# Attention and a gated FFN in one kernel: scaled values made with the second score unit, evenly spaced attention bursts, and a start with the second batch's attention moved into the first FFN chunk

## The chip, the cores and the metric

The kernel runs on one core of a Trainium2 chip. The metric is the device time of one execution in microseconds (us). Several executions of each kernel are timed, and one execution of each is profiled. The span of a profile, from the first to the last instruction, is about 2 us shorter than the time of the same execution.

## The reference

```python
# attention, per batch b and head h: B = H = 8, S = 576, D = 64
scores = q @ k^T / sqrt(D) + cum[i] - cum[j]     # cum = cumsum(log(clip(f)))
attn   = softmax(scores, causal)
o      = attn @ v
# FFN on x = o with heads side by side: 4608 tokens x 512
out = (sigmoid(x @ w_gate) * (x @ w_val)) @ w_out     # 512 -> 1536 -> 512
```

The kernel writes exp(cum[i] - cum[j]) as a factor for i, which cancels in the softmax, and a factor g[j] = exp(-cum[j]), shifted by a constant. It multiplies v by g; the result, `vg`, is "the scaled values" of this text.

## The kernel before

Heads are worked on in pairs; there are 32 pairs, four to a batch. A pair's scores are computed transposed (keys on partitions) in four units A, B, C and D, because the causal triangle is cut into pieces that fit PSUM banks. Each unit goes through PE (scores), ACT (exp) and POOL (causal mask). Then the AV stage on PE multiplies by `vg` and, for the row sums, by `g`.

```python
def Q_exp(p, u, sc):                      # unit u of pair p, scores in banks sc, sc+1
    e = esb.tile(...)
    nc.scalar.activation(e, ps[:, sc:sc + 2, 0:w], Exp, scale=scale)
    nc.gpsimd.affine_select(out=m, in_=m, ...)            # mask, on POOL

def vg_step(p):
    nc.gpsimd.tensor_tensor(out=vg, in0=vb[...], in1=g_bf[...], op=mult)   # on POOL

def AV_mm(p, b0, b1, b2):                 # outputs in b0, b1; row sums in b0, b2
    av(p, CH0, b0, C0, False)             # needs vg, eA, eC
    av(p, CH0, b0, 0, True); av(p, CH1, b2, 0, True)
    av(p, CH1, b1, 0, False)              # needs eB, eD as well
def norm_r(...)   # DVE: transposes of the row sums, reciprocal, transpose back
def norm_m(...)   # DVE: xT = output (b0, b1) * R, the "output multiply"
```

PE does the FFN in chunks of 512 tokens, nine in all. A chunk is 36 groups of four matmuls: 24 groups for gate and value, then 12 for the output. Between groups PE takes up attention work of the next batch, in "bursts" (`later` is emptied after the next FFN group):

```python
def burst1(p):
    Q_mm(p, "C", 2); Q_mm(p, "A", 0); Q_exp(p, "C", 2)
    later.append(lambda: Q_exp(p, "A", 0))
def burst2(p):
    Q_mm(p, "B", 2); Q_mm(p, "D", 0); Q_exp(p, "B", 2)
    later.append(lambda: (Q_exp(p, "D", 0), vg_step(p)))      # vg last
def burst3(p):
    T_step(p + 1, "k", 3, nc.scalar.copy); T_step(p + 1, "q", 4, nc.scalar.copy)
    AV_mm(p, 0, 1, 2); norm_r(p, 0, 1, 2)
    later.append(lambda: norm_m(p, 0, 1, 2))

# start: pairs 0..3 (batch 0) without FFN; early_pair(p) also transposes pair p+1
early_pair(0); load_w1(1); early_pair(1)
load_qk(1, 0, 1); load_v(1, 0)
early_pair(2); load_w1(2); early_pair(3); early_av(3)
burst1(4); flush(); burst2(4); flush()
load_qk(1, 1, 1); load_v(1, 1)
bursts = {0: burst3, 4: burst1, 7: burst2}   # position within nine FFN groups
for c in range(NTC):
    for s, grp in enumerate(ffn_groups(c)):
        ...                                   # loads; burst if s % 9 is in bursts
        grp(); flush()
```

So the FFN groups between bursts number 4 (AV to burst 1), 3 (burst 1 to burst 2) and 2 (burst 2 to AV).

The softmax here doesn't subtract the row's maximum and nothing guards it: scores larger than these inputs give would overflow.

Of the kernel before, what the change touches and what calls it, by code (L numbers as in the profile page):

```python
# [15 lines left out]
def kernel(  # L16
# [11 lines left out]
    nc = tc.nc  # L28
    B, H, S, D = q.shape
# [6 lines left out]
    HPAIR = H // 2  # L36
# [47 lines left out]
    def load_qk(b, hf, npiece):  # L84
        key = (b, hf)
        qt = qk_pool.tile([QP, 4, TPP * D], BF16, tag="qt", name="qt")
        kt = qk_pool.tile([QP, 4, TPP * D], BF16, tag="kt_in", name="kt_in")
        w = 4 // npiece
        for s in range(npiece):
            for src, dst in ((q, qt), (k, kt)):  # L90
                hs = slice(4 * hf + w * s, 4 * hf + w * s + w)
                nc.gpsimd.dma_start(
                    dst[:, w * s:w * s + w, :],
                    src[b, hs].rearrange("h (p t) d -> p h (t d)", t=TPP))
        qtiles[key], ktiles[key] = qt, kt

    def load_v(b, hf):
        vb = vbs[(2 * b + hf) % NVB]
        for h in range(4):
            nc.sync.dma_start(  # L100
                vb[:, 0:NJT - 1, h, :],
                v[b, 4 * hf + h, 0:(NJT - 1) * NP, :].rearrange("(t p) d -> p t d", p=NP))
        nc.sync.dma_start(
            vb[0:TAIL, NJT - 1, :, :],
            v[b, 4 * hf:4 * hf + 4, (NJT - 1) * NP:S, :].rearrange("h p d -> p h d"))

    def load_w1(gi):
        cs = slice(gi * 512, gi * 512 + 512)
        for src, dst in ((moe_w_gate, wg_bf), (moe_w_val, wv_bf)):
            nc.gpsimd.dma_start(dst[:, :, cs],  # L110
                                src.rearrange("(m p) c -> p m c", p=NP)[:, :, cs])

    def load_w2(gi):
        nc.gpsimd.dma_start(
            wo_bf[:, 4 * gi:4 * gi + 4, :],
            moe_w_out.rearrange("(m p) c -> p m c", p=NP)[:, 4 * gi:4 * gi + 4, :])
# [3 lines left out]
    later = []  # L120

    def flush():
        while later:
            later.pop(0)()

    def half_of(p):
        b, a = divmod(p, HPAIR)
        return b, a // 2, 2 * (a % 2)

    def T_step(p, which, bk, copy):  # L130
        b, hf, ho = half_of(p)
        src = (qtiles if which == "q" else ktiles)[(b, hf)]
        bank = ps[:, bk, 0:S // 2].bitcast(BF16)
        for t in range(TPP):
            for h in range(2):
                nc.tensor.transpose(  # L136
                    bank[64 * h:64 * h + 64, t * QP:(t + 1) * QP],
                    src[:, ho + h, t * D:(t + 1) * D], ident_bf[0:QP, 0:QP])
        if which == "q":
            dst = asb.tile([128, S], BF16, tag="qT", name="qT")  # L140
        else:
            dst = kts[p % NKT]
        st[p, which] = dst
        copy(dst[:, 0:S].rearrange("p (n t) -> p n t", t=TPP),  # L144
             bank.rearrange("p (t n) -> p n t", t=TPP))
# [10 lines left out]
    def Q_mm(p, u, sc):  # L156
        qT, kT = st[p, "q"], st[p, "k"]
        for jt, i0, i1, c in UNITS[u]:
            for h in range(2):
                hp = slice(64 * h, 64 * h + 64)  # L160
                nc.tensor.matmul(ps[:, sc + h, c:c + i1 - i0],  # L161
                                 kT[hp, jt * NP:(jt + 1) * NP], qT[hp, i0:i1],
                                 start=True, stop=True)

    def Q_exp(p, u, sc):
        w = UW[u]
        e = esb.tile([128, 2, 512], BF16, tag="e" + u, name="e" + u)
        st[p, u] = e
        nc.scalar.activation(e[:, :, 0:w], ps[:, sc:sc + 2, 0:w], ACTF.Exp, scale=scale)  # L169
        if u == "A":  # L170
            m = e.rearrange("p h (x c) -> p h x c", x=2)[:, :, :, 0:NP]
            pat = [[0, 2], [0, 2], [1, NP]]
        elif u == "B":
            m = e[0:TAIL, :, 320:320 + TAIL]
            pat = [[0, 2], [1, TAIL]]
        else:
            m = e[:, :, 0:NP]
            pat = [[0, 2], [1, NP]]
        nc.gpsimd.affine_select(out=m, in_=m, compare_op=ALU.is_ge, fill=0.0,  # L179
                                base=0, pattern=pat, channel_multiplier=-1)  # L180

    def vg_step(p):
        b, hf, ho = half_of(p)
        vb = vbs[(2 * b + hf) % NVB]
        vg = asb.tile([128, NJT, 2, D], BF16, tag="vg", name="vg")
        st[p, "vg"] = vg
        nc.gpsimd.tensor_tensor(  # L187
            out=vg, in0=vb[:, :, ho:ho + 2, :],
            in1=g_bf[:, :, 2 * p:2 * p + 2].unsqueeze(3).to_broadcast([128, NJT, 2, D]),
            op=ALU.mult)  # L190
# [19 lines left out]
    def AV_mm(p, b0, b1, b2):  # L210
        av(p, CH0, b0, C0, False)
        av(p, CH0, b0, 0, True)
        av(p, CH1, b2, 0, True)
        av(p, CH1, b1, 0, False)

    def norm_r(p, b0, b1, b2):
        NB = S // 32
        Z = nsb.tile([128, S], FP32, tag="Z", name="Z")
        nc.vector.transpose(Z[:, 0:C0], ps[:, b0, 0:C0])  # L219
        nc.vector.transpose(Z[:, C0:S], ps[:, b2, 0:C1])  # L220
        r = nsb.tile([128, NB], FP32, tag="r", name="r")
        nc.vector.reciprocal(r, Z.rearrange("p (n c) -> p n c", c=32)[:, :, 0])
        R = nsb.tile([128, S], FP32, tag="R", name="R")
        nc.vector.transpose(R.rearrange("p (n c) -> p n c", c=32),  # L224
                            r.unsqueeze(2).to_broadcast([128, NB, 32]))
        st[p, "R"] = R

    def norm_m(p, b0, b1, b2):
        b, a = divmod(p, HPAIR)
        psf = ps.rearrange("p b c -> p (b c)")  # L230
        o = b0 * 512 + C0
        nc.vector.tensor_tensor(out=xT[:, a, b * S:(b + 1) * S], in0=psf[:, o:o + S],  # L232
                                in1=st[p, "R"], op=ALU.mult)


    def early_pair(p):
        Q_mm(p, "A", 0)
        Q_exp(p, "A", 0)
        Q_mm(p, "C", 2)
        Q_exp(p, "C", 2)  # L240
        T_step(p + 1, "q", 4, nc.scalar.copy)
        T_step(p + 1, "k", 7, nc.vector.tensor_copy)
        vg_step(p)
        if p:
            early_av(p - 1)
        Q_mm(p, "B", 0)
        Q_exp(p, "B", 0)
        Q_mm(p, "D", 2)
        Q_exp(p, "D", 2)

    def early_av(p):
        AV_mm(p, 5, 6, 7)
        norm_r(p, 5, 6, 7)
        norm_m(p, 5, 6, 7)


    def burst1(p):
        if p >= NPAIR:
            return
        Q_mm(p, "C", 2)  # L260
        Q_mm(p, "A", 0)
        Q_exp(p, "C", 2)
        later.append(lambda: Q_exp(p, "A", 0))

    def burst2(p):
        if p >= NPAIR:
            return
        Q_mm(p, "B", 2)
        Q_mm(p, "D", 0)
        Q_exp(p, "B", 2)  # L270
        later.append(lambda: (Q_exp(p, "D", 0), vg_step(p)))

    def burst3(p):
        if p >= NPAIR:
# [55 lines left out]
    nc.sync.dma_start(f_nat, f.rearrange("b h s -> (b h) s"))  # L330
    load_qk(0, 0, 2)
    make_identity(nc, ident_bf)
    make_identity(nc, ident_f)
    load_qk(0, 1, 2)
    for i in range(NVB):
        nc.vector.memset(vbs[i][TAIL:NP, NJT - 1, :, :], 0.0)
    for i in range(NKT):
        nc.vector.memset(kts[i][:, S:SPAD], 0.0)
    nc.vector.memset(g_bf[TAIL:NP, NJT - 1, :], 0.0)
    load_v(0, 0)  # L340
    load_v(0, 1)

    nc.vector.tensor_scalar(out=f_nat, in0=f_nat, scalar1=1e-4, scalar2=1.0,
                            op0=ALU.max, op1=ALU.min)
# [10 lines left out]
    nc.vector.tensor_copy(g_bf[:, 0:NJT - 1, :], gps[:, 0:NJT - 1, :])  # L355
    nc.vector.tensor_copy(g_bf[0:TAIL, NJT - 1, :], gps[0:TAIL, NJT - 1, :])

    load_w1(0)
    early_pair(0)
    load_w1(1)  # L360
    early_pair(1)
    load_qk(1, 0, 1)
    load_v(1, 0)
    early_pair(2)
    load_w1(2)
    early_pair(3)
    early_av(3)
    burst1(4)
    flush()
    burst2(4)  # L370
    flush()
    load_qk(1, 1, 1)
    load_v(1, 1)

    bursts = {0: burst3, 4: burst1, 7: burst2}
    for c in range(NTC):
        P = HPAIR * (c + 1)
        for s, grp in enumerate(ffn_groups(c)):
            if c == 0 and s in (2, 5, 8):
                load_w2(s // 3)  # L380
            if s in ((2, 20) if c else (12, 26)) and c + 2 < B:
                load_qk(c + 2, int(s >= 20), 1)
                load_v(c + 2, int(s >= 20))
            x, y = divmod(s, 9)
            if y in bursts:
                bursts[y](P + x + (y > 0))
            grp()
            flush()

# [29 lines left out]
```

## Time and profile before

| | before |
|---|---|
| median time, 4 runs | 451.72 us (449.46 to 453.02) |
| span of the profiled run | 447.9 us |
| first FFN matmul | 46.93 us |
| a chunk with four pairs of attention | 48.38 us |
| a chunk without attention | 31.08 us |

From the page of the kernel before: the first line is an engine's busy time, its share and its instructions; the others show the busy share in 40 equal slices of the span, in tenths, and the granted TensorE clock in tenths of full speed.

```profile
PE 396.7 (89%) x3349; PEld 197.7 (44%) x3349; DVE 167.9 (37%) x283; ACT 221.0 (49%) x335; POOL 126.9 (28%) x213
...
PE   4726998999899989999899989998999988999996
...
PEclk9968899999999999999999999999999999999999
```

PE is the engine that bounds the kernel from the fifth slice on, but it keeps dropping from 9 to 8. The four stretches below are the start, chunk 0, chunk 1 and a chunk without attention (after the times: busy us of PE, PEld, DVE, ACT and POOL with instruction counts, then granted clock, DMA share and GB/s).

```profile
0.00:46.93 46.93, 25.36 (x349) 18.12 (x350) 19.36 (x39) 23.19 (x31) 29.03 (x52) 0.86 1.06 178
46.93:95.38 48.45, 44.78 (x402) 21.98 (x400) 18.72 (x31) 26.26 (x40) 17.37 (x28) 1.00 0.59 100
95.38:143.76 48.38, 44.71 (x402) 22.00 (x400) 19.02 (x33) 26.26 (x40) 14.57 (x24) 1.00 0.36 70
381.75:412.83 31.08, 31.08 (x146) 14.07 (x145) 8.26 (x12) 9.55 (x16) 0.00 (x0) 1.00 0.09 34
```

In chunk 1 PE is idle for 48.38 - 44.71 = 3.67 us, and no other engine is over 55% busy. What PE waits for after 47 us is in the list of waits: `vg`, 25.8 us in 27 waits, the longest 1.5 us. What PE waits for after 47 us is in the list of waits (total us, number of waits, longest): first for the matmul row, then, from the same list for the weight-load row, the same wait.

```profile
PE ps L206 <- POOL vg L187: 25.8, 27, 1.5
...
PEld L206 <- POOL vg L187: 29.8, 27, 1.8
```

One pair in the timeline (start, duration, engine, line, operation; in brackets the idle time before it and what ended it) shows why `vg` is late.

```profile
150.36 0.64 POOL L179 TENSOR_SCALAR_AFFINE_SELECT eA<-eA 128x512 bf16<-128x512 bf16 x1 [1.18 <-ACT eA L169]
...
152.70 0.41 POOL L179 TENSOR_SCALAR_AFFINE_SELECT eD<-eD 128x256 bf16<-128x256 bf16 x1 [0.30 <-ACT eD L169]
...
153.03 0.42 PE L136 MATMUL ps<-ident_bf,qt 96*64 96x96 bf16 x12
153.08 1.27 POOL L187 TENSOR_TENSOR vg<-vb_89,g_bf 128x640 bf16<-128x640 f32 x1
...
154.40 0.30 PE L206 MATMUL ps<-eA,vg 128*64 128x256 bf16 x2 [0.95 <-POOL vg L187]
```

POOL had nothing to do between the mask of eA (done at 151.00) and the mask of eB (152.11), but `vg` stands in its queue behind the last mask. The Trainium skill's page "Perfetto Trace Analysis", section "Tensor Engine Instruction (MATMUL, LD_WEIGHTS)", calls the execution queues of ACT, DVE and GpSimd (POOL here) strictly first in, first out, and the trace agrees: the 1.11 us of idle time ahead of the mask of eB went unused, and `vg` ran last. PE is through with its transposes at 153.45 and waits for `vg` until 154.40. The chain of waits over another pair shows the same from the other side (start, us, what):

```profile
104.21 0.39 POOL eD L179
104.60 1.25 POOL vg L187
105.85 0.04 issue
105.89 1.56 PE ps L206 x28
```

The mask of eD and `vg` lie on the chain that ended last, and the AV stage that follows takes 1.56 us in it.

### The profile page before, as it was taken

Reading aid. Unit: us, or ns where it says so; the run is one execution under the profiler, and the core shown is the slowest. Engines: PE = TensorE matmul, PEld = TensorE weight load, DVE = VectorE, ACT = ScalarE, POOL = GpSimd, SP = SyncE. Lnnn points to the kernel's source line nnn. Section 1 sums busy time; section 2 is a strip of 40 time slices with the busy share of each in tenths; the row PEclk is TensorE's granted clock in tenths of the full one; section 3 lists DMA queues with packets and bytes.
Section 4 is the critical chain, followed back from the end, with each engine's and each line's share of the span. In section 5 each row is a group of like instructions: output and inputs, shape, how many; then the busy total and the mean of one; then the engine's idle time right before and its main releaser. Section 6 shows DMA issues by size and latency. Waiting matters only on the chain.

```text
span 447.9 us, 8234 instructions
## 1 busy us (share of the span) xinstructions
PE 396.7 (89%) x3349; PEld 197.7 (44%) x3349; DVE 167.9 (37%) x283; ACT 221.0 (49%) x335; POOL 126.9 (28%) x213
## 2 busy tenths in 40 slices
PE   4726998999899989999899989998999988999996
PEld 2514444444444444444444444444444444444442
DVE  4524444234432444244423443244324442340330
ACT  5634455455555555455555554555545542332321
POOL 7753342432323233232323232323221121000000
PEclk9968899999999999999999999999999999999999
DMA  9998890573313703181317230370410001101002
GB/s 167 196 194 163 127 174 1 101 138 70 44 34 91 133 8 55 72 152 31 55 48 144 63 51 28 93 134 5 67 58 25 0 1 48 47 1 70 23 2 94
DMA packets 61061, 33.70 MB, mean 75 GB/s; under 512 B 39456, under 2 KB 56352, under 8 KB 61024
## 3 DMA queue, kind: packets, MB, share of 16 engines
q0 software_dynamic: 17616, 14.16, 21.7%
q1 hardware_dynamic: 43408, 19.03, 16.6%
q8 instruction: 26, 0.43, 0.4%
q14 instruction: 11, 0.09, 0.1%
HBM read 37.90 MB, written 9.44 MB: 106 GB/s over the span
## 4 chain that ended last, share of the span: by engine, by line
PE 66%; POOL 12%; ACT 8%; issue 8%; DMA 4%; DVE 1%; POOLq 0%; ACTq 0%
PE ps L300 33%; PE ps L315 16%; PE ps L206 11%; POOL vg L187 8%; PE ps L161 5%; ACT eB L169 4%; DMA kt_in<-in_k_dram 4%; ACT eC L169 2%; POOL eB L179 2%; POOL eD L179 2%; ACT eA L169 2%; POOL eA L179 1%; PE ps L136 1%; DVE kt_87 L144 1%; DMA out_dram<-ob 0%
## 5 line engine op out<-in xcount | busy, mean ns | idle before, releaser
L305 ACT ACTIVATE sg<-ps 128x512 bf16<-128x512 f32 x108 | 64.5, 597 | 120.8 <-PE ps L300 120.8
L307 DVE SCALAR_TENSOR_TENSOR gv<-sg,ps 128x512 bf16<-128x512 bf16 x108 | 74.3, 688 | 122.8 <-PE ps L300 120.9
L300 PE MATMUL ps<-xT,wg_bf 128*128 128x512 bf16 x432 | 111.3, 380 | 0.0
L300 PE MATMUL ps<-xT,wv_bf 128*128 128x512 bf16 x432 | 111.1, 380 | 0.0
L315 PE MATMUL ps<-wo_bf,gv 128*128 128x512 bf16 x432 | 99.2, 380 | 0.0
L300 PEld LDWEIGHTS <-wv_bf 128*128 128x128 bf16 x432 | 40.6, 98 | 49.4 <-issue 2.4
L315 PEld LDWEIGHTS <-gv 128*128 128x128 bf16 x432 | 40.1, 98 | 49.0 <-issue 3.2
L300 PEld LDWEIGHTS <-wg_bf 128*128 128x128 bf16 x432 | 39.4, 98 | 48.7 <-issue 4.1
L179 POOL TENSOR_SCALAR_AFFINE_SELECT eC<-eC 128x256 bf16<-128x256 bf16 x32 | 13.1, 409 | 163.1 <-ACT eC L169 163.1
L219 DVE STREAM_TRANSPOSE Z<-ps 128x256 f32<-128x256 f32 x32 | 14.4, 449 | 117.0 <-PE ps L206 117.0
L319 ACT ACTIVATE ob<-ps 128x512 f32<-128x512 f32 x36 | 21.5, 597 | 58.4 <-PE ps L315 55.1
L206 PE MATMUL ps<-eA,vg 128*64 128x192 bf16 (+1 forms) x128 | 18.3, 280 | 28.3 <-POOL vg L187 27.4
L206 PEld LDWEIGHTS <-vg 128*64 128x64 bf16 x448 | 23.4, 114 | 34.9 <-POOL vg L187 31.5
L169 ACT ACTIVATE eC<-ps 128x896 bf16<-128x896 f32 x32 | 29.3, 915 | 14.1 <-PE ps L161 14.1
L169 ACT ACTIVATE eB<-ps 128x768 bf16<-128x768 f32 x32 | 25.9, 811 | 20.1 <-PE ps L161 20.1
L169 ACT ACTIVATE eA<-ps 128x896 bf16<-128x896 f32 x32 | 29.3, 914 | 1.4 <-PE ps L161 1.4
L179 POOL TENSOR_SCALAR_AFFINE_SELECT eA<-eA 128x512 bf16<-128x512 bf16 x32 | 20.5, 641 | 23.4 <-ACT eA L169 23.4
L224 DVE STREAM_TRANSPOSE R<-r 128x576 f32<-128x576 f32 x32 | 24.9, 778 | 1.1
L232 DVE TENSOR_TENSOR xT<-ps,R 128x576 bf16<-128x576 f32 x32 | 24.2, 756 | 2.6
L136 PE MATMUL ps<-ident_bf,qt 96*64 96x96 bf16 x384 | 14.6, 216 | 11.0 <-DMA qt<-in_q_dram 5.7
L206 PEld LDWEIGHTS <-g_bf 128*64 128x64 bf16 x448 | 22.5, 116 | 3.2 <-issue 1.3
L144 ACT COPY qT<-ps 128x576 bf16<-128x576 bf16 x32 | 20.8, 651 | 5.3 <-PE ps L136 5.3
(55 smaller groups left out, 352.1 us busy)
## 6 DMA issues: line engine op xcount, KB each, us to landing
out_dram<-ob SPq DMA_DIRECT2D x36, 256.0 KB, 2.0
qt<-in_q_dram POOLq DMA_DIRECT2D x14, 288.0 KB, 5.5
kt_in<-in_k_dram POOLq DMA_DIRECT2D x14, 288.0 KB, 6.9
vb_89<-in_v_dram SPq DMA_DIRECT2D x24, 128.0 KB, 5.6
vb_90<-in_v_dram SPq DMA_DIRECT2D x20, 128.0 KB, 5.6
vb_91<-in_v_dram SPq DMA_DIRECT2D x20, 128.0 KB, 5.8
wg_bf<-in_moe_w_gate_dram POOLq DMA_DIRECT2D x3, 512.0 KB, 10.2
wv_bf<-in_moe_w_val_dram POOLq DMA_DIRECT2D x3, 512.0 KB, 12.7
```

The source lines that it names most:

```text
L144: copy(dst[:, 0:S].rearrange("p (n t) -> p n t", t=TPP), bank.rearrange("p (t n) -> p n t", t=TPP))
L161: nc.tensor.matmul(ps[:, sc + h, c:c + i1 - i0], kT[hp, jt * NP:(jt + 1) * NP], qT[hp, i0:i1], start=True, stop=True)
L169: nc.scalar.activation(e[:, :, 0:w], ps[:, sc:sc + 2, 0:w], ACTF.Exp, scale=scale)
L179: nc.gpsimd.affine_select(out=m, in_=m, compare_op=ALU.is_ge, fill=0.0, base=0, pattern=pat, channel_multiplier=-1)
L187: nc.gpsimd.tensor_tensor(out=vg, in0=vb[:, :, ho:ho + 2, :], in1=g_bf[:, :, 2 * p:2 * p + 2].unsqueeze(3).to_broadcast([128, NJT, 2, D]), ...
L206: nc.tensor.matmul(ps[64 * h:64 * h + 64, bank, off + oc:off + oc + w], lhsT, st[p, u][:, h, c:c + w], start=(x == 0), stop=(x == n - 1), ...
L224: nc.vector.transpose(R.rearrange("p (n c) -> p n c", c=32), r.unsqueeze(2).to_broadcast([128, NB, 32]))
L232: nc.vector.tensor_tensor(out=xT[:, a, b * S:(b + 1) * S], in0=psf[:, o:o + S], in1=st[p, "R"], op=ALU.mult)
L300: nc.tensor.matmul(ps[:, bk, :], w[:, mt, ft * NP:(ft + 1) * NP], xT[:, mt, t0:t0 + TCH], start=(mt == 0), stop=(mt == NMT - 1))
L305: nc.scalar.activation(sg, ps[:, bk, :], ACTF.Tanh, scale=0.5)
L307: nc.vector.scalar_tensor_tensor(out=gv[:, ft, :], in0=hold["sg"], scalar=1.0, in1=ps[:, bk, :], op0=ALU.add, op1=ALU.mult)
L315: nc.tensor.matmul(ps[:, bk, :], gv[:, ft, tt * NP:(tt + 1) * NP], wo_bf[:, ft, :], start=(ft == 0), stop=(ft == NFT - 1))
```

## The change

The change is meant to take `vg` off the critical path by queueing it on POOL right behind the mask of eA (the second score unit that a pair puts on PE), to space the bursts of chunks 1 and later evenly (three FFN groups between two bursts, but for one gap of two and one of four), and to start the FFN sooner: the second batch's attention is no longer begun ahead of the FFN but in the later part of chunk 0, one burst every two groups. Loads are reordered to suit (the first weights sooner, the loads of later batches at later groups of a chunk), and those of v for batch 1 are held back by tiny memsets on POOL ("gates").

```diff
+    def load_v(b, hf, gate=None):
+        if gate is not None:
+            for h in range(4):
+                gate.memset(vb[0:1, 0, h, 0:1], 0.0)
 ...
 def early_pair(p):
-        T_step(p + 1, "q", 4, nc.scalar.copy)
-        T_step(p + 1, "k", 7, nc.vector.tensor_copy)
+        if p + 1 < HPAIR:
+            T_step(p + 1, "q", 4, nc.scalar.copy if p % 2 else nc.vector.tensor_copy)
+            T_step(p + 1, "k", 7, nc.vector.tensor_copy)
 ...
+    def burst0(p):
+        T_step(p, "k", 3, nc.scalar.copy)
+        T_step(p, "q", 4, nc.scalar.copy)
 def burst1(p):
-        later.append(lambda: Q_exp(p, "A", 0))
+        later.append(lambda: (Q_exp(p, "A", 0), vg_step(p)))
 def burst2(p):
-        later.append(lambda: (Q_exp(p, "D", 0), vg_step(p)))
+        later.append(lambda: Q_exp(p, "D", 0))
 ...  (the identities, the first loads and the loads of later batches are moved)
     load_qk(1, 0, 1)
-    load_v(1, 0)
+    load_v(1, 0, nc.gpsimd)
 ...
+    load_qk(1, 1, 1)
+    load_v(1, 1, nc.gpsimd)
     early_av(3)
-    burst1(4)
-    flush()
-    burst2(4)
-    flush()
-    load_qk(1, 1, 1)
-    load_v(1, 1)
-    bursts = {0: burst3, 4: burst1, 7: burst2}
+    # chunk 0:  burst0 at group 9, then bursts 1, 2, 3, 1, ... at
+    pos = [10, 12, 14, 16, 18, 20, 22, 24, 26, 28, 30, 32]
+    # chunks 1 and later:
+    pos = [0, 3, 6, 9, 12, 15, 18, 21, 24, 26, 29, 32]
```

More of the change, by code (lines that the diff above doesn't have):

```diff
@@ L95, in load_qk @@
         qtiles[key], ktiles[key] = qt, kt
-    def load_v(b, hf):
+    def load_v(b, hf, gate=None):
         vb = vbs[(2 * b + hf) % NVB]
+        if gate is not None:
+            for h in range(4):
+                gate.memset(vb[0:1, 0, h, 0:1], 0.0)
         for h in range(4):
@@ L332 @@
     make_identity(nc, ident_bf)
+    load_qk(0, 1, 2)
     make_identity(nc, ident_f)
-    load_qk(0, 1, 2)
     for i in range(NVB):
@@ L341 @@
     load_v(0, 1)
+    load_w1(0)
     nc.vector.tensor_scalar(out=f_nat, in0=f_nat, scalar1=1e-4, scalar2=1.0,
@@ L356 @@
     nc.vector.tensor_copy(g_bf[0:TAIL, NJT - 1, :], gps[0:TAIL, NJT - 1, :])
-    load_w1(0)
     early_pair(0)
@@ L366, with positions @@
     early_pair(3)
+    load_qk(1, 1, 1)
+    load_v(1, 1, nc.gpsimd)
     early_av(3)
-    burst1(4)
-    flush()
-    burst2(4)
-    flush()
-    load_qk(1, 1, 1)
-    load_v(1, 1)
-    bursts = {0: burst3, 4: burst1, 7: burst2}
+    def positions(c):
+        P = HPAIR * (c + 1)
+        if c == 0:
+            at = {9: (burst0, P)}
+            pos = [10, 12, 14, 16, 18, 20, 22, 24, 26, 28, 30, 32]
+        else:
+            at = {}
+            pos = [0, 3, 6, 9, 12, 15, 18, 21, 24, 26, 29, 32]
+        for x, s in enumerate(pos):
+            at[s] = ((burst1, burst2, burst3)[x % 3], P + x // 3)
+        return at
     for c in range(NTC):
-        P = HPAIR * (c + 1)
+        at = positions(c)
         for s, grp in enumerate(ffn_groups(c)):
@@ L380 @@
                 load_w2(s // 3)
-            if s in ((2, 20) if c else (12, 26)) and c + 2 < B:
-                load_qk(c + 2, int(s >= 20), 1)
-                load_v(c + 2, int(s >= 20))
-            x, y = divmod(s, 9)
-            if y in bursts:
-                bursts[y](P + x + (y > 0))
+            if s in ((8, 26) if c else (18, 30)) and c + 2 < B:
+                load_qk(c + 2, int(s >= 24), 1)
+                load_v(c + 2, int(s >= 24))
+            if s in at:
+                fn, p = at[s]
+                fn(p)
             grp()
```

## The prediction

> **What bounds it now.** TensorE: PE is busy 89% of 447.9 us (the page), and 66% of the chain that ended last. Four parts, from the timeline and the table by stretches:
> - Start, 0 to 46.9 us: the first FFN matmul begins at 46.93. The largest idle is 24.1 to 31.8: pair 3's step transposes pair 4, whose q and k were issued at 19.2 and 19.9 and land 10.6 and 11.9 us later. PE waits 5.7 + 1.3 us; the granted clock is 0.73 to 0.78 from 20 to 47 us. Pair 4's score units then run with no FFN work between them (38.9 to 44.1).
> - FFN: a chunk without attention takes 31.08 us; nine take 279.7.
> - 27 pairs within chunks 0 to 6: a chunk with four takes 48.4, so 4.33 us a pair. Of that PE waits for the scaled values (vg on POOL): 25.8 us in 27 waits, 0.95 each. That list has nothing else for PE after 47 us.
> - Tail: 3.8 us.
>
> **Why vg is late.** It is queued on POOL behind the pair's last mask: in one pair eD's mask ends at 153.11, vg at 154.35, while PE could begin at about 153.45. The change queues vg behind the mask of eA, which ended at 151.0: done by about 152.3. Its 1.27 us is moved into POOL idle time, not removed.
>
> **Steps.**
> 1. Steady chunks: the vg wait goes, 0.95 x 27 = 25.8 us, all on the critical path: 3.37 a pair. New waits: the output multiply ends about 2.0 us after AV and frees the banks; three FFN groups (2.59 us) cover it, two (1.73) do not. Estimate 0.5 us a chunk, 3 us in six.
> 2. Start: no batch-1 transposes before the FFN. The 7 us DMA wait and pair 4's unhidden 8 us go. By before's durations: AV of pair 2 at 24.1, vg of pair 3 done at 28.8, AV of pair 3 to 31.0, 2.05 us of normalisation, FFN at about 33.3.
> 3. Pair 4 moves into chunk 0: 28 pairs there, +3.4 us. With two groups between bursts, exp of eA ended 2.97 us after its burst began, but the next burst wants its bank after 2.5; with the normalisation about 1.1 us a pair, plus 0.6 for the first copies: 5 us of new waits.
> 4. q copies on DVE, order of identities, gates: under 1 us.
>
> Sum: 33.3 + 279.7 + 28 x 3.37 (94.4) + 3 + 5 + 3.8 = 419 us span; the timed median lies 4 us above the span of before: **423 us**. Range 415 to 432. Chances: faster 0.97, same 0.02, slower 0.01.
>
> **The skill.** "TensorE: Matmul & The Clock Gate", What's actually happening: the default state is throttled, activity releases it. The trace agrees: after the idle at 24 to 30 us a 320-wide AV matmul pair spans 0.50 us instead of 0.30.
>
> **What would show it.** PE's waits for vg after the start under 3 us (wrong above 10). First FFN matmul at 31 to 36 us. Chunks 1 to 6 at 44.5 to 45.5 us; chunk 0 about 50.
>
> **What would make it wrong.** Chunk 0: q/k/v of batch 1, gated later and sharing the queues with all of w_out, may land after their bursts. The early pairs may be bound by v of half 1 (vg of pair 2 started only at 23.2). ACT may fall behind in chunk 0.

## The result, and the profile after

| | before | after |
|---|---|---|
| median time, 4 runs each | 451.72 us | 414.34 us (412.48 to 416.30) |
| span of the profiled run | 447.9 us | 413.7 us |
| first FFN matmul | 46.93 us | 33.53 us |
| chunk 0 | 48.45 us | 50.71 us |
| chunk 1 | 48.38 us | 44.07 us |
| a chunk without attention | 31.08 us | 31.08 us |

The kernel is faster: ratio 0.9178, with a 95% interval of 0.9107 to 0.9248. All ratios here are the mean time of one kernel's fast runs over that of the other's in the same rounds, so not quite the ratio of the medians quoted. A chunk is counted from its first gate matmul to that of the next chunk, both read from the timeline.

The prediction had the direction and the order of size right, but the median lies 0.7 us below its range and 8.7 us below its central value.

The page of the kernel after, with the lines that answer to those of before:

```profile
PE 394.2 (95%) x3349; PEld 195.5 (47%) x3349; DVE 169.2 (41%) x284; ACT 220.5 (53%) x334; POOL 126.0 (30%) x221
...
PE   3868999999999999999999999999999999999996
...
PEclk9986999999999999999999999999999999999999
```

PE's busy time hardly moved (396.7 to 394.2 us); its idle time went, and the row of 9s has no holes after the start. The start, chunk 0, chunk 1 and a chunk without attention by stretches:

```profile
0.00:33.53 33.53, 19.45 (x262) 13.71 (x263) 18.85 (x36) 17.44 (x22) 27.16 (x57) 0.92 1.15 189
33.53:84.24 50.71, 49.05 (x431) 23.67 (x430) 19.19 (x32) 27.28 (x42) 14.99 (x25) 0.96 0.71 122
84.24:128.31 44.07, 44.07 (x403) 21.77 (x401) 19.09 (x32) 26.26 (x41) 14.45 (x24) 1.00 0.41 86
347.60:378.68 31.08, 31.08 (x146) 14.11 (x144) 8.26 (x12) 9.55 (x16) 0.00 (x0) 1.00 0.09 34
```

In chunk 1 PE is now busy in all 44.07 us. In the list of waits of the whole run, the largest PE waits all belong to the start, and from 84 us to the end the list for the matmul row is empty:

```profile
PE ps L139 <- DMA qt<-in_q_dram: 5.3, 1, 5.3
PE ps L308 <- DVE xT L235: 2.0, 1, 2.0
PE ps L209 <- POOL vg L190: 2.0, 1, 2.0
```

A pair in the timeline: `vg` (87.39 to 88.65) now runs in the gap behind the mask of eA, and PE goes from its transposes to AV without a wait.

```profile
86.78 0.64 POOL L182 TENSOR_SCALAR_AFFINE_SELECT eA<-eA 128x512 bf16<-128x512 bf16 x1 [1.00 <-ACT eA L172]
87.39 1.26 POOL L190 TENSOR_TENSOR vg<-vb_90,g_bf 128x640 bf16<-128x640 f32 x1
...
89.00 0.41 POOL L182 TENSOR_SCALAR_AFFINE_SELECT eD<-eD 128x256 bf16<-128x256 bf16 x1
...
90.31 0.42 PE L139 MATMUL ps<-ident_bf,qt 96*64 96x96 bf16 x12
...
90.57 0.28 PE L209 MATMUL ps<-eA,vg 128*64 128x256 bf16 x2
```

The chain of waits over the same pair has only PE in it, and the AV stage takes 1.37 us in it where it took 1.56:

```profile
87.41 2.70 PE ps L308 x12
90.10 0.63 PE ps L139 x24
90.73 1.37 PE ps L209 x28
```

This is not a slower AV stage before. From its first matmul to the next FFN matmul the timeline has 154.40 to 155.90, or 1.50 us, before and 90.57 to 92.04, or 1.47 us, after. The chain counts from the end of the work before it, and when PE did not wait, the first AV matmul began 0.16 us ahead of the modelled end of the transposes (90.57 against 90.31 + 0.42 = 90.73).

Not all is well at the start of chunk 0. The first three FFN groups run at about half the clock, the next stretch at the full one:

```profile
33.53:38.35 4.82, 4.82 (x12) 1.67 (x12) 0.69 (x1) 0.60 (x1) 0.63 (x1) 0.53 1.25 198
38.35:43.60 5.25, 5.25 (x25) 2.25 (x23) 2.03 (x3) 1.79 (x3) 0.00 (x0) 1.00 1.25 195
```

Twelve matmuls took 4.82 us there; a group takes 31.08 / 36 = 0.863 us elsewhere, so three should take 2.59 us.

### The profile page after: what moved, and what is told of

The parts are those of the page before. It is cut to its first block, busy times and chain, and to the rows that moved or that the text cites. A ratio compares the mean times of both kernels' runs of the same rounds, so it can differ in the third digit from the quotient of the medians.

```text
span 413.7 us, 8263 instructions
## 1 busy us (share of the span) xinstructions
PE 394.2 (95%) x3349; PEld 195.5 (47%) x3349; DVE 169.2 (41%) x284; ACT 220.5 (53%) x334; POOL 126.0 (30%) x221
## 4 chain that ended last, share of the span: by engine, by line
PE 86%; POOL 3%; DMA 3%; issue 3%; SPq 2%; ACT 2%; DVE 1%; POOLq 0%; ACTq 0%; DVEq 0%
PE ps L308 45%; PE ps L323 22%; PE ps L209 9%; PE ps L164 6%; PE ps L139 4%; DMA vb_90<-in_v_dram 3%; SPq L103 2%; POOL vg L190 1%; ACT sg L313 0%; ACT eA L172 0%; POOL eC L182 0%; POOL eA L182 0%; POOL qt L92 0%; POOL kt_in L92 0%; ACT eD L172 0%
## 5 line engine op out<-in xcount | busy, mean ns | idle before, releaser
L308 PE MATMUL ps<-xT,wg_bf 128*128 128x512 bf16 x432 | 112.6, 384 | 2.0 <-DVE xT L235 2.0
L172 ACT ACTIVATE eD<-ps 128x640 bf16<-128x640 f32 x32 | 22.5, 705 | 0.0
L164 PE MATMUL ps<-qT,kt_88 64*128 64x448 bf16 (+3 forms) x192 | 18.5, 285 | 1.9 <-ACT eB L172 1.2
L164 PE MATMUL ps<-qT,kt_87 64*128 64x64 bf16 (+3 forms) x192 | 18.5, 290 | 1.9 <-ACT eA L172 0.8
```

The costliest lines, as they stand in the source:

```text
L164: nc.tensor.matmul(ps[:, sc + h, c:c + i1 - i0], kT[hp, jt * NP:(jt + 1) * NP], qT[hp, i0:i1], start=True, stop=True)
L172: nc.scalar.activation(e[:, :, 0:w], ps[:, sc:sc + 2, 0:w], ACTF.Exp, scale=scale)
L308: nc.tensor.matmul(ps[:, bk, :], w[:, mt, ft * NP:(ft + 1) * NP], xT[:, mt, t0:t0 + TCH], start=(mt == 0), stop=(mt == NMT - 1))
```

## The experiments

Twelve kernels were run. All gave correct results.

### The place of vg and the spacing, taken apart

Two parts of the change act on the same wait: with `vg` early it is ready before AV asks; with wider spacing AV asks later. Four kernels take them apart. The first is the kernel before with only the two lines of `vg` changed:

```diff
 # before, burst1
-        later.append(lambda: Q_exp(p, "A", 0))
+        later.append(lambda: (Q_exp(p, "A", 0), vg_step(p)))
 # burst2
-        later.append(lambda: (Q_exp(p, "D", 0), vg_step(p)))
+        later.append(lambda: Q_exp(p, "D", 0))
```

> Kernel before with one edit: vg is queued on POOL after the mask of eA instead of after the mask of eD; nothing else changes. Theory T (the whole cost of the late vg is the wait plus a slower restart: in the trace of before an AV stage takes 1.56 us after the wait, in the trace of after 1.38 us): 27 x (0.95 + 0.18) = 30 us go, about 422 us, ratio 0.933, no PE wait for vg after the start. Rival as in the prediction (only the listed wait goes, and 0.5 us of new waits a chunk come): 23 us go, about 429 us.

Measured: 419.98 us median (418.40 to 420.44) against 451.69 us for before in the same rounds, ratio 0.9283 (0.9247 to 0.9320). That is 31.7 us gained by moving one instruction per pair, and the rival's 429 us is ruled out. Chunk 1 takes 43.96 us. The list of PE's waits from 85 to 400 us, here in full, has none for `vg`:

```profile
PE ps L300 <- issue: 1.9, 12, 0.2
PE ps L315 <- DVE Z L220: 0.8, 5, 0.2
PE ps L315 <- issue: 0.2, 1, 0.2
```

The second is the kernel after with those two lines undone:

```diff
 # after, burst1 and burst2: vg_step(p) back behind Q_exp(p, "D", 0)
```

> Kernel after with vg put back behind the mask of eD; even spacing and start kept. Theory S (the even spacing gives vg one FFN group, 0.86 us, more, and so by itself hides most of the wait of 0.95 us): chunks 1 to 6 lose 0.1 to 0.6 us a pair, chunk 0 with two groups between units and AV loses about 1.1 us a pair; in all 6 to 12 us over after, 421 to 426 us. Rival (the place of vg is what matters, the spacing does nothing): 27 x 1.1 = 30 us over after, about 444 us.

Measured: 432.50 us (431.99 to 433.32), ratio to before 0.9575 (0.9540 to 0.9610). That is 18 us over after: more than my 6 to 12 us, less than the rival's 30. Chunk 1 takes 46.08 us. The list of waits from 84 us on shows that about half of the pairs from there on still wait:

```profile
PE ps L209 <- POOL vg L190: 8.2, 12, 1.3
```

So the even spacing hides about half of a late `vg`. I had put too little on chunk 0 (54.61 us, where two groups still lie between burst 2 and AV) and on the pairs that still wait in later chunks.

The third keeps `vg` early and takes the spacing back; the fourth takes both back, so that of the change only the start, the loads and the denser chunk 0 are left:

```diff
 # after, chunks 1 and later (both kernels; the fourth with vg late as well)
-            pos = [0, 3, 6, 9, 12, 15, 18, 21, 24, 26, 29, 32]
+            pos = [0, 3, 5, 9, 12, 14, 18, 21, 23, 27, 30, 32]
```

> Kernel after with vg early, but in chunks 1 and later the spacing of before (4, 3 and 2 groups between bursts instead of 3, 3, 3). If the early vg alone removes the wait, the time is that of after within 1.5 us (413 to 416 us), and chunks 1 to 6 stay at 44.0 us. If the spacing is needed as well (masks of eB and eD or copies late with two groups), 4 us or more over after.

Measured: 413.52 us (411.61 to 415.30), ratio 0.9138 (0.9100 to 0.9176): the same as after. Chunk 1 takes 43.96 us, 0.1 us less than with even spacing.

> Kernel after with both undone in chunks 1 and later: vg late and spacing 4, 3, 2. What is left of the change is the start, the loads and the second batch in chunk 0. Theory: a steady chunk is again 48.4 us, 6 x 4.4 = 26 us and some 4 us in chunk 0 over after, about 444 us, so the start alone is worth 6 to 8 us against before. Rival (the start is worth its 13.4 us earlier first FFN matmul): about 438 us.

Measured: 446.37 us (444.62 to 448.06), ratio 0.9866 (0.9816 to 0.9917). Chunk 1 takes 48.69 us. The start with all that goes with it is worth about 5.3 us (451.69 - 446.37; by the interval 4 to 8; 6 to 8 were expected), though its first FFN matmul, at 34.02 us, comes 12.9 us sooner than before. The rest is given back later: chunk 0 takes 54.13 us where it took 48.45, and chunk 6 takes 48.22 us where it took 44.32, because pair 4, and with it every later pair, has moved back in the order.

The length of chunk 1 in the four cases:

| | spacing 3, 3, 3 | spacing 4, 3, 2 |
|---|---|---|
| vg early | 44.07 us | 43.96 us |
| vg late | 46.08 us | 48.69 us |

With `vg` early, the spacing does nothing. With `vg` late, the spacing is worth 2.6 us a chunk. The parts are substitutes, not a sum. The place of `vg` by itself (31.7 us) and the start by itself (5.3 us) do add up, to 37.0 us, where the whole change measured 37.4; with an uncertainty of 2 us and more in the second part, so close a match is in part luck. A check in the same rounds: with the new start, the place of `vg` is worth 446.37 - 413.52 = 32.9 us.

### The new wait that did not come

The prediction charged 0.5 us a chunk for the output multiply that holds up the next burst. None of it appeared. In the kernel after, the output multiply of the pair shown above ran from 93.36 to 94.12 us, and AV had ended at 92.10, so the 2.0 us were right. Three groups follow there; the critical place is the one gap of two groups in each chunk, and PE does not wait there either. What was wrong must be whom the multiply holds up. The test puts unit A ahead of C in burst 1:

```diff
-        Q_mm(p, "C", 2)
         Q_mm(p, "A", 0)
+        Q_mm(p, "C", 2)
```

> Kernel after with the two score units of burst 1 in the other order on PE: A (banks 0 and 1) ahead of C (banks 2 and 3). The prediction said that the output multiply, done 2.0 us after AV, holds up the next burst by 0.5 us a chunk and more in chunk 0; none came. Theory O: the multiply reads banks 0 and 1 only, C goes first and gives it 0.25 us more. Then with A first PE waits for the multiply (or the activation behind it): 0.2 to 0.5 us a pair where two groups lie between (chunk 0, and once in each later chunk), 2 to 5 us in all. Rival: the multiply is done in time in either order, and no wait comes.

Measured (one look): ten waits for the output multiply, 3.2 us in all, from the list of waits after 33 us:

```profile
PE ps L164 <- DVE xT L235: 3.2, 10, 0.3
```

Nine of the ten come where two groups lie between AV and burst 1: three in chunk 0, one in each of chunks 1 to 6. Chunk 1 takes 44.36 us instead of 44.07. The multiply reads banks 0 and 1. Unit C is written to banks 2 and 3, of which AV had used only bank 2, for row sums that a short transpose reads first. So C may go ahead, and its matmuls give the multiply the time that it still needs, but hardly more: in the two-group gap of chunk 1 in the kernel after, C began at 115.85 us, the multiply ended at 116.10, and A began at 116.16. The order C, A was in the kernel before, and I had overlooked what it does.

### The start

The first FFN groups ran at half the clock just after two PE waits of 2 us. The next kernel fills these waits with idle matmuls:

```diff
+    def warm(n):        # results unused, bank 4 is free here
+        for _ in range(n):
+            nc.tensor.matmul(ps[:, 4, 0:TCH], ident_bf, xT[:, 0, 0:TCH], start=True, stop=True)
 ...
+    warm(7)
     early_av(3)
+    warm(7)
```

> Kernel after with 7 idle matmuls (512 wide, result unused, to a free bank) in each of PE's two waits just ahead of the FFN (1.96 us for vg of pair 3, 2.0 us for its normalisation). Runs of after split into two at 412.5 (mean granted clock 0.999) and two at 416.2 (0.987). Theory C (these waits let the clock drop, and the first three FFN groups run at half speed, 4.82 us instead of 2.6): all runs near 412.5, none at 416; no group of the first FFN stretch over 1.1 us. Rival (the split has another cause, such as the DMA): two kinds of runs as before, or all slower by the added work.

Measured: 414.47 us (412.60 to 417.23), ratio 0.9172 (0.9138 to 0.9207): no gain, and not the single kind of run that was expected. The first groups ran at the full clock, as the stretch from the first FFN matmul on shows:

```profile
36.85:39.50 2.65, 2.65 (x13) 1.23 (x13) 0.65 (x1) 0.60 (x1) 0.37 (x1) 1.00 1.09 154
```

Chunk 0 took 48.47 us instead of 50.71, which fits the 2.2 us of the half clock. That the idle matmuls did this is not shown. In the profile of the kernel with all copies of q on ACT (below), which has none, PE waited as long ahead of the first FFN matmul (2.06 us) as in after (2.00), and still that group took 1.02 us and not 1.87, and chunk 0 took 48.77:

```profile
33.68 1.02 PE L308 MATMUL ps<-xT,wg_bf 128*128 128x512 bf16 x4 [2.06 <-DVE xT L235]
```

In both profiles the half clock fell a few us sooner, on AV of pair 2 (28.01 to 31.42 us here, 25.28 to 28.69 there; in after 31.26 to 38.08). And the spread stayed: the four runs took 412.6, 413.8, 415.1 and 417.2 us, so the two kinds of runs of after (412.5 us at a mean granted clock of 0.999, and 416.2 at 0.987 to 0.988) are not explained by the first groups alone. In the profiled run the FFN began only at 36.85 us, since AV of pair 2 waited 2.6 us for its `vg`. How far the run-to-run spread comes from the clock and how far from when loads land stays open.

Two small parts of the start were undone, in one look each. First the gates:

```diff
-    load_v(1, 0, nc.gpsimd)    # and load_v(1, 1, nc.gpsimd)
+    load_v(1, 0)               # and load_v(1, 1)
```

> Kernel after without the small memsets on POOL that hold back the loads of v of batch 1. If the gates matter for the start, v of batch 1 takes DMA time from batch 0 and from the first weights: vg of pair 2 later than 22.9 us and the first FFN matmul 1 us or more later than 33.5. If not, it stays within 33 to 34 us and the time within 1 us of 412.5 or 416.2.

Measured: 416.54 us, one run; first FFN matmul at 34.85 us. In after the `vg` of pair 2 began at 22.94 us; without the gates POOL waited for it until 25.46:

```profile
25.46 1.26 POOL L190 TENSOR_TENSOR vg<-vb,g_bf 128x640 bf16<-128x640 f32 x1 [3.50 <-PE ps L164]
```

The releaser named there cannot be meant, since `vg` reads nothing of the scores; the last load of v for that pair landed at 25.25 us (22.73 in after). In this one look the FFN began 1.3 us later without the gates. But the same load landed at 26.67 us in the profile of the idle matmuls above and at 22.7 to 24.3 us in the others with the gates and this order of loads; in before, without gates and in another order, it landed at 22.98. So neither the effect nor the worth of the gates is shown.

Then the copies of q:

```diff
-        T_step(p + 1, "q", 4, nc.scalar.copy if p % 2 else nc.vector.tensor_copy)
+        T_step(p + 1, "q", 4, nc.scalar.copy)
```

> Kernel after with all copies of q in the early pairs on ACT, as in before. The move to DVE helps pair 0 (ACT is busy there) and hurts pair 2, where the copy of k queues behind it and PE waited 1.0 us for it. Expected: that wait is 0.2 us or less, the first FFN matmul within 1 us of 33.5 us: about zero in the time. If the move was needed, the start is 1 us or more later.

Measured: 414.44 us, one run; first FFN matmul at 33.68 us, and the longest wait for a copy of k was 0.5 us instead of 1.0 (I had expected 0.2 or less).

### Tries at a better kernel

Four kernels rework the start further. The common parts: nine matmuls of the first three FFN groups (the three contraction tiles that do not need pair 3) go ahead of pair 3's normalisation, and AV of pair 3 goes to banks 0, 1 and 4.

```diff
-    early_av(3)
+    AV_mm(3, 0, 1, 4); norm_r(3, 0, 1, 4); norm_m(3, 0, 1, 4)
 ...
+        def begin():
+            for ft, w, kind in ((0, wg_bf, "g"), (0, wv_bf, "v"), (1, wg_bf, "g")):
+                bk = begun[ft, kind] = next_bank()
+                for mt in range(NMT - 1):      # the last mt follows in g1
+                    nc.tensor.matmul(ps[:, bk, :], w[...], xT[:, mt, ...], start=(mt == 0), stop=False)
```

The first try also put pair 4's transposes ahead of the first FFN groups and its bursts from group 1 on:

> An attempt at a better kernel: after, with the last third of w1 issued behind pair 3's vg, AV of pair 3 in banks 0, 1 and 4, so that nine matmuls of the first three FFN groups and the transposes of pair 4 fill the wait for the normalisation, and pair 4 to 7 spread evenly over chunk 0. If the waits ahead of the FFN and the two-group spacing of chunk 0 are what is left: first FFN matmul at 30 to 31 us, chunk 0 at 44 to 47 us, time 405 to 409 us. If DMA bounds chunk 0 (v of the second half of batch 1 landed at 52.7 us), PE waits move there and it gains under 3 us.

Measured: 410.78 us (408.90 to 414.30), ratio 0.9113 (0.9063 to 0.9164). The FFN began at 29.59 us, a little sooner than expected, but the time missed 405 to 409 us, and chunk 0 took 48.80 us, not 44 to 47: burst 1 of pair 4 was too early, PE waited 0.3 to 0.7 us three times for copies and activations, and the clock fell to half for two groups after that.

The second try moves the weight loads behind the early pairs and starts pair 4 at group 3:

> The better kernel, next try: the first w1 part is issued only behind pair 0's work on POOL, the second behind pair 1's, q, k and v of batch 1 behind pair 2's; the FFN's first nine matmuls still fill the wait for pair 3; pair 4 starts at group 3 and the bursts of chunk 0 are two and three groups apart. If v of half 1 (landed at 22.7 to 23.4 us, vg of pair 2 waited for it) holds the early pairs, the first FFN matmul comes at 25 to 28 us; chunk 0 loses the 2 us of waits and cold matmuls of the last try: 404 to 408 us. If the chain of activations holds them, it stays near 29 us: 407 to 410 us.

Measured: 410.47 us (409.12 to 410.67), ratio 0.9090 (0.9064 to 0.9116). The first guess was wrong: the last load of v of half 1 landed at 15.33 us instead of 22.73, yet the FFN did not begin sooner than in the first try. Chunk 0 did get shorter, but the time met neither of the two ranges. The stretches are the start and chunk 0:

```profile
0.00:30.65 30.65, 19.21 (x261) 13.61 (x262) 16.05 (x32) 17.97 (x23) 23.29 (x48) 0.94 1.06 171
30.65:76.94 46.29, 45.33 (x426) 22.50 (x431) 21.00 (x36) 26.84 (x42) 18.63 (x34) 1.00 0.92 157
```

The third try adds idle matmuls from the first microsecond on and after each early pair:

> The last one with idle matmuls on a cleared tile: nine before the first q lands, one after each of the first transposes, three small ones after each early pair. In all traces so far the early pairs ran at half clock until about 17 us. If a clock raised sooner shortens the early pairs, the first FFN matmul comes 1 to 3 us sooner than without, and the time falls as much. If activations and DMA bound them, nothing is gained, or the added work costs up to 1 us.

Measured: 409.81 us (408.13 to 410.91), ratio 0.9075 (0.9038 to 0.9113).

```profile
0.00:27.05 27.05, 20.26 (x285) 12.50 (x285) 16.33 (x33) 17.76 (x23) 23.33 (x48) 1.00 1.09 178
27.05:77.90 50.85, 47.24 (x426) 22.87 (x431) 20.99 (x36) 26.94 (x42) 18.63 (x34) 0.97 0.90 151
```

The start is 3.6 us shorter in the profiled runs. The low clock did cost time among the early pairs: in one and the same AV stage a pair of 320-wide matmuls took 0.52 us in the second try (at 15.74 us) and 0.33 us here (at 13.98), and pair 1's last exp ended 4.85 us after pair 0's instead of 6.65. The granted clock of the profile does not show this: it reads 1.00 from 5 to 17 us in both, since its first record comes at 17.24 us in the second try, so the digits of PEclk for the first 17 us of the pages above say nothing. The gain did not reach the time (1 to 3 us were expected): chunk 0 grew by 4.6 us: PE waited 2.1 us for k of batch 1, whose load did not come sooner, and two groups at half clock followed. The last try put pair 4 at group 8 and later to avoid that:

> The last try at a better kernel: as the warm one (FFN from 27.05 us, but chunk 0 took 50.9 us: PE waited 2.1 us for k of batch 1 and ran two groups at half clock after it), with pair 4's transposes at group 8 and its bursts from group 10, every two groups, as in after, and the loads of batch 1's q, k, v issued behind pair 3's vg. Expected: no PE wait on DMA after the FFN has begun, FFN from 26 to 27 us, chunk 0 47 to 48 us, 405 to 408 us. If DMA bounds the first 55 us whatever the order, the wait moves to a later load (v of batch 1) and the time stays at 409 to 411 us.

Measured: 410.29 us (409.88 to 411.16), ratio 0.9098 (0.9082 to 0.9115). There was no wait on DMA after the FFN had begun, but the FFN began at 29.16 us, not 26 to 27, and chunk 0 took 48.98 us, not 47 to 48, with the waits of two-group spacing. All four tries end within 1 us of each other; they are about 4 us, or 1%, faster than after (409.8 to 410.8 against 414.3 us), but their intervals overlap that of after (0.9107 to 0.9248), and they were not timed in the same rounds as after. So it is not shown that they are faster than after. In the profiled runs, what one of them gains in the start chunk 0 gives back.

## Why the prediction was wrong

The direction and the main mechanism (the `vg` wait) were right. Two steps failed: the new waits for the output multiply did not come, and the step from span to time was 3.4 us too long; two more terms of chunks 1 to 6 were mis-sized. The terms of the prediction's sum against the profiled run of after:

| term | predicted | measured |
|---|---|---|
| first FFN matmul | 33.3 us | 33.53 us |
| chunk 0 (31.08 + 4 x 3.37 + 5) | 49.6 us | 50.71 us |
| chunks 1 to 6 (6 x (31.08 + 4 x 3.37 + 0.5)) | 270.4 us | 263.36 us |
| chunks 7 and 8, tail | 66.0 us | 66.1 us |
| span | 419.2 us | 413.7 us |
| time over span | 4 us | 2.4 us |
| median against the profiled run | 0 us | -1.8 us |

- **"The vg wait goes, 0.95 x 27 = 25.8 us": right in mechanism, mis-sized.** A wait costs more than the matmul row shows. In the spacing of before, a chunk with four pairs takes 48.38 us with the wait and 43.96 us without it (the `vg` experiment on before), so a pair loses 4.42 / 4 = 1.105 us. The list of waits for the weight-load row had that number all along: 29.8 / 27 = 1.10 us. A second pair of kernels agrees: from the third kernel to the fourth (`vg` early and late, both in the spacing of before), 24 waits come to 24.6 us in the matmul row and 28.2 us in the weight-load row, and chunks 1 to 6 grow by 29.0 us. The matmul row counts only from the modelled end of the last matmul on. The Trainium skill's page "TensorE: Matmul & The Clock Gate", section "What happens when you issue a matmul", says that in a stream of matmuls the drain of one overlaps the fill of the next; in the section "Single matmul latency" it puts the part of one matmul's latency that does not depend on its width, and which it calls the drain, at about 175 ns. An estimate from that page is thus 0.17 us more for each stall. The trace agrees: without a stall AV begins 0.16 us ahead of the end of the transposes, after a stall it cannot, and 1.105 - 0.955 = 0.15 us over all pairs. The "slower restart" of the first experiment's expectation is this lost overlap; the size was right, the name was not. With a pair at 3.25 us ((44.07 - 31.08) / 4) instead of 3.37, 24 pairs account for 2.9 us.
- **"New waits: ... 0.5 us a chunk, 3 us in six": wrong.** No such wait came. The step that failed is "the output multiply ends about 2.0 us after AV and frees the banks": it frees only the banks of A, and burst 1 sends C ahead of A. With A first the waits came, 3.2 us in ten. The size was off too: there is one two-group gap in a chunk, so even with A first it was 44.36 - 44.07 = 0.29 us a chunk, 1.7 us in six and not 3.
- **A pair counted in full that is not.** Chunk 6 has no next pair to transpose after its last one, and chunk 7's burst does not exist; it took 42.98 us where chunks 1 to 5 took 44.07. That is 1.1 us. These three items, 2.9 + 3 + 1.1, make up the 7.0 us of chunks 1 to 6.
- **Chunk 0: right total from wrong parts, so luck.** I charged 5 us of waits. The list from 38 us on shows 1.2 us for exp of eA and 0.2 us for the copy of q. Two AV stages, whose masks stood on POOL behind two DMA issues, took 2.1 and 1.7 us to the next FFN group where the others took 1.5. The largest item I did not foresee: the half clock at its start, 4.82 - 2.59 = 2.2 us. These come to 4.4 us; the chunk is 50.71 - 31.08 - 4 x 3.37 = 6.2 us over its sum without waits, so not all of it is accounted for.
- **The start: right.** 33.3 us predicted, 33.53 measured, with the chain given: `vg` of pair 3, AV, normalisation. That it fits within 0.3 us is luck: in kernels with nearly the same start it came between 32.22 and 36.85 us. That it would be worth less than its 13 us, since pair 4 moves and does not vanish, was in the sum and was confirmed: 5.3 us alone.
- **From span to time.** I added 4 us, the distance from the median of before to the span of one profiled run. But that profiled run was itself fast for its kernel (449.59 us, where the timed runs took 449.46 to 453.02). The time of an execution over its own span was 1.7 us there and 2.4 us after. Half of the runs of after took 412.5 us, and the profiled one was of the slower half. These two items make up 3.4 us of the miss. With the 5.5 us of the span (7.0 too many in chunks 1 to 6, 1.5 too few elsewhere) that is the whole miss (8.9 us, since the sum before rounding was 423.2).
- **What could have made it wrong did not.** Loads of batch 1 were in time in chunk 0, and PE never waited more than 0.4 us at a time for ACT. The third risk was there as in before, whose durations the sum had used: `vg` of pair 2 began at 22.94 us, when v of half 1 had landed at 22.73.

The evenly spaced bursts, which the change names first after `vg`, are not a cause of the gain: with `vg` early, after runs as fast without them.

## What to carry to other kernels

When a small operation stands in an in-order queue behind work that it does not depend on, look for where its inputs are ready first, and queue it in the idle gap there; this was worth 31.7 us of 37.4 here and moved one instruction per pair. Read the cost of a stalled matmul stream from the weight-load row or from the length of a stage with and without the stall, since the matmul row leaves out the overlap that a stall destroys (about 0.15 us each here). Before charging a new wait, check bank by bank which instruction it would hold up, and before adding up two fixes of one wait, ask whether either would do alone.

## What the Trainium skill lacked or had wrong

- "Perfetto Trace Analysis", section "Tensor Engine Instruction (MATMUL, LD_WEIGHTS)", says that the end of a matmul in the profile is an estimate, but not that the idle time in front of the next matmul is then too short as the cost of a stall. Here it was 0.955 us a pair in the matmul row, 1.10 us in the weight-load row, and 1.105 us in the time.
- "TensorE: Matmul & The Clock Gate", section "HAM oscillation", gives the rule as no idle gaps of PE over about 3.4 us. In the kernel after, no wait of PE between 20 and 33.5 us was longer than 2.0 us, and still the clock was at half from 31.26 to 38.08 us, and the first twelve FFN matmuls ran at a granted clock of 0.53 and took 4.82 us instead of 2.59. The page's own section "What's actually happening", by which the clock follows how busy PE has been of late, fits this better: from 27.85 to 31.26 us PE was busy for 1.45 of 3.41 us. A threshold is not shown: from 28.41 to 31.82 us in the fourth kernel (`vg` late, spacing 4, 3, 2) PE was busy just as long, and the clock stayed full.
